# A short piece of rows moves from slot 23 to slot 10, and TensorE's loop is split in two around it

## The chip, the cores and the metric

The kernel runs on one core of one Trainium2 chip. The metric is device time in microseconds (us) for one execution. Four executions of the kernel before took 488.97, 487.42, 485.47 and 479.20 us, a median of 486.44. One further execution was profiled: it took 480.64 us, of which the span from the first to the last instruction is 478.9 us.

## The reference

A grouped 1x1 convolution over a 512 x 512 image of 192 channels in bfloat16: four groups of 48 channels, each multiplied by its own 48 x 48 matrix. With a kernel size of 1 there is no padding and one term in the sum:

```
x: (1, 512, 512, 192) bf16        w: (1, 1, 4, 48, 48) bf16
xg  = x.reshape(1, 512, 512, 4, 48)
out = einsum('bhwgc,gcd->bhwgd', xg, w[0, 0]).reshape(1, 512, 512, 192)
```

So 262,144 pixels of 192 channels are read, 100.7 MB, and as many bytes are written. Each pixel is independent of every other, which leaves the order free.

## The kernel before, in words

**Pieces and slots.** The pixels are cut into pieces (`plan_pieces`, L73). A full piece holds 128 rows, one per partition, and a number of columns; a column is one pixel of 192 channels, 384 bytes. Most pieces have 80 columns, so each partition's part is one contiguous run of 30,720 bytes. The work unit is a *group* of 4 columns, and two groups make a *pair*; there are 513 groups and 257 pairs. Pieces lie in 26 *slots*: slot 0 holds three small pieces (8, 24 and 48 columns), slots 1 to 22 and slot 24 one piece of 80 columns each, slot 25 one of 68, and slot 23 the *short piece*. That one has 64 columns and only 120 rows: partitions 16 to 19 and 48 to 51 are left out of it (`PARTIAL`, L40), so nothing is read into them or written from them. It is made of five blocks of rows: two of 16 rows, moved by the same queues as the other pieces (SP for loads, ACT for stores), and three of 44, 12 and 32 rows, moved by POOL. Ahead of the first two of these, POOL issues a tiny *fill* transfer (L234) into a tile that nobody reads.

**The rings.** Loaded columns lie in `ring`, three slots of 80 columns. A slot's load is issued when TensorE has transposed the piece that lay there three slots earlier (`freed`, L210; waits at L238 for POOL and L258 for SP). Results lie in `oring`, 280 columns, written round and round. Where a full piece would run over the end, its store is split in two; the short piece is not split: where it doesn't fit before the end, it starts at column 0 (L108). Before ScalarE writes a group into `oring`, it waits until the store that last read those columns has landed (`landed`, L356, called at L384).

**The engines.** TensorE transposes each group's 4 columns with six 128 x 128 transposes (L291, into `xT_ps`), one pair ahead of the matmuls that multiply them with the block-built weights `wt` (L311, six for each group, into `o_ps`). VectorE copies a pair's transposes to SBUF (L349). ScalarE copies each group's result to `oring` (L386) and issues the store of a finished piece (L367) when it comes to the second group after it; then for the short piece it also tells POOL to issue its three stores (L369). SP issues all other loads (L260) in the order of the pieces. The tail is cut finer: pieces with fewer than 240 columns behind them are stored in parts of 40, the last one in parts of 24, 20, 16 and 8.

**TensorE's program.** Its code is written out pair by pair, apart from one hardware loop (L333). A loop body is 60 groups, or 30 pairs: three slots, after which all buffers and semaphores repeat. `loop_span` (L117) finds the run of 80-column pieces that begins with slot 1; the loop starts at pair 10 and makes 7 rounds, and pairs 220 to 256 follow, written out. The short piece ends the run, since its loads have other semaphores. The programs of VectorE and ScalarE are written out in full.

Of the kernel before, what the change touches and what calls it, by code (L numbers as in the profile page):

```python
# [24 lines left out]
BIG = 80  # L25
SLOTS = 3
RCOLS = SLOTS * BIG
# [5 lines left out]
NXP = 4  # L33
NXS = 3
NOB = 4
NTOK = 6
# [5 lines left out]
    ("pool", 52, 44, 11), ("pool", 20, 12, 3), ("pool", 96, 32, 8),  # L42
)
PARTIAL_COLS = 64
PARTIAL_SLOT = 23

FILL_ROWS = 5
FILL_BEFORE = (2, 3)
# [24 lines left out]
def plan_pieces(npix):  # L73
    few = PARTIAL_COLS * sum(b[2] for b in PARTIAL)
    partial = npix >= few + 128 * BIG * PARTIAL_SLOT
    cols = (npix - few * partial) // 128
    assert cols % 4 == 0
    head = list(HEAD) if cols >= sum(HEAD) else []
    mid = cols - sum(head)
    slots = [[(BIG, FULL)]] * (mid // BIG) + ([[(mid % BIG, FULL)]] if mid % BIG else [])  # L80
    if head:
        slots.insert(0, [(s, FULL) for s in head])
    if partial:
        slots.insert(PARTIAL_SLOT, [(PARTIAL_COLS, PARTIAL)])
    pieces, g, pix = [], 0, 0
    for n, parts in enumerate(slots):
        c = n % SLOTS * BIG
        for s, blocks in parts:
            pieces.append(Piece(len(pieces), n, c, g, s, blocks, pix))
            c, g, pix = c + s, pieces[-1].g1, pieces[-1].pix_end  # L90
    assert pix == npix
    return pieces
# [21 lines left out]
    return stores  # L114


def loop_span(pieces, ng):  # L117

    body = RCOLS // 4
    a = next((p.g0 for p in pieces if p.slot == 1), ng)  # L120
    b = a
    for p in pieces:
        if p.slot >= 1 and p.g0 == b and p.full and p.size == BIG:
            b = p.g1

    rounds = max(0, (b - a - 2) // body)
    return a, body, rounds


def bass_standalone__grouped__vision_kernel(nc, x, w, out):  # L130
# [5 lines left out]
    pieces = plan_pieces(npix)  # L136
# [2 lines left out]
    store_of = {g: s for s in stores for g in range(s.g0, s.g1)}  # L139
    NG = pieces[-1].g1  # L140
    NP = (NG + 1) // 2
    LA, LB, LR = loop_span(pieces, NG)
    assert LA % 2 == 0 and LB % (2 * NXS) == 0 and LB % (2 * NTOK) == 0 and LB % NXP == 0

    xf = x.rearrange("b h w c -> (b h w) c")
    of = out.rearrange("b h w c -> (b h w) c")
# [2 lines left out]
    def groups(pair):  # L149
        return range(2 * pair, min(2 * pair + 2, NG))  # L150
# [21 lines left out]
    with ExitStack() as es:  # L172
# [27 lines left out]
        def columns(g):  # L200
            p = piece_of[g]
            at = p.at + 4 * (g - p.g0)
            return ring[:, at * C:(at + 4) * C]
# [58 lines left out]
        @block.tensor  # L262
        def _(pe):

            def build_weights():
                pe.wait_ge(e_sem, 1)
                pe.wait_ge(w_sem, 16)
                last = None
                for (tc, r, g, c0_) in WBLOCKS:
                    s0 = ESHIFT - r  # L270
                    col = WOFF[tc] + c0_
                    last = pe.matmul(o_ps[:, NOB - 1, col:col + CG], lhsT=esel[:, s0:s0 + 128],  # L272
                                     rhs=w_sb[:, g, :], start=True, stop=True, skip_group_check=True)
                last.then_inc(wb_sem, 1)

            def transposes(pair):
                todo = []
                for g in groups(pair):
                    p = piece_of[g]
                    if g % 2 and pair:  # L280
                        pe.wait_ge(e_done[(pair - 1) % NTOK], 1)
                    if g == p.g0:
                        keys = [ld_key[p.i, n] for n in range(len(p.blocks))]
                        for key in keys:
                            pe.wait_ge(ld_sem[key], 16)
                        todo += keys if p.full else []
                    xg = columns(g)
                    for ul in range(2):
                        for tc in range(3):
                            j = ul * 3 + tc  # L290
                            last = pe.transpose(xT_ps[:, g % NXP, j * 128:(j + 1) * 128],  # L291
                                                xg[:, j * 128:(j + 1) * 128], ident[:])
                            if todo and 0 < j < 5:
                                last.then_inc(ld_sem[todo.pop(0)], -16)
                assert not todo
                last.then_inc(t_done, 1)

            def matmuls(pair):
                if pair + 1 == NP or len(groups(pair + 1)) < 2:
                    pe.wait_ge(e_done[pair % NTOK], 1)  # L300
                for g in groups(pair):
                    xs = xT_sb[pair % NXS][:, g % 2 * 2 * UC:(g % 2 + 1) * 2 * UC]
                    if g >= 2:
                        pe.wait_ge(fa_done[(g - 2) % (2 * NTOK)], 1)
                    last = None
                    for ul in range(2):
                        v = 2 * g + ul
                        for tc in range(3):
                            j = ul * 3 + tc
                            c0_, c1_ = COLR[tc]  # L310
                            last = pe.matmul(o_ps[:, v % NOB, c0_:c1_], lhsT=xs[:, j * 128:(j + 1) * 128],  # L311
                                             rhs=wt[:, WOFF[tc]:WOFF[tc] + (c1_ - c0_)],
                                             start=(tc == 0), stop=(tc == 2), skip_group_check=True)
                            if j == 2 and g >= 2:
                                last.then_inc(fa_done[(g - 2) % (2 * NTOK)], -1)
                            if j == 1 and g % 2 == 0:
                                last.then_inc(e_done[pair % NTOK], -1)
                    last.then_inc(mm_done, 1)

            def step(pair):  # L320
                if pair + 1 < NP:
                    transposes(pair + 1)
                matmuls(pair)

            build_weights()
            pe.wait_ge(id_sem, 1)
            transposes(0)
            pe.wait_ge(wc_sem, 1)
            first = LA // 2 if LR > 1 else NP
            for pair in range(first):  # L330
                step(pair)
            if LR > 1:
                with pe.Fori(0, LR):  # L333
                    for pair in range(first, first + LB // 2):
                        step(pair)
                for pair in range(first + LR * LB // 2, NP):
                    step(pair)

        @block.vector
        def _(dve):  # L340
# [80 lines left out]
```

## Time and profile before

| | us |
|---|---|
| median of four executions | 486.44 |
| lowest, highest | 479.20, 488.97 |
| the profiled execution | 480.64 |
| its span | 478.9 |
| busy TensorE matmul, ScalarE, VectorE in it | 427.7, 388.9, 246.3 |
| bytes moved, mean rate over the span | 201.65 MB, 421 GB/s |
| median from issue to landing: an 80-column load, an 80-column store | 26.2, 45.1 |

The profile page cuts the span into 40 slices of 12.0 us. A digit is the busy share of a slice in tenths, and 9 stands for 90% or more. TensorE's matmuls are pipelined and the ends of their records are modelled, so its busy time is no measure of how close it is to its peak. The row of the DMA engines is the mean over sixteen. A wait in the views below names the engine and line that stood idle, what it was released by, the total in us, the number of such waits and the longest. In the view of stages each engine's busy time comes with its count of instructions, and "PEclk" is the share of TensorE's clock that was granted.

### The profile page before, as it was taken

The page shows a single profiled execution, that of the slowest core. Times are in us where ns is not written, and L with a number is a line of the kernel's source. Part 1 is how long each engine was busy: PE and PEld are TensorE (multiplying, and loading weights), DVE is VectorE, ACT ScalarE, POOL GpSimd, SP SyncE. Part 2 cuts the span into 40 slices and gives each one's busy share as a digit, 9 for nine tenths or more (in the row PEclk, how much of TensorE's full clock was granted, in tenths as well). Part 3 has the DMA queues.
Part 4 walks back from the last instruction along what each step waited for, and adds up shares of the span by engine and source line. Part 5 has one row for each costly group of instructions (what it writes and reads, how often), then busy time and mean ns, then how long its engine had stood idle before and what let it go on. Part 6 is the DMA issues. An engine that isn't in the chain of part 4 may idle for free.

```text
span 478.9 us, 13531 instructions
## 1 busy us (share of the span) xinstructions
PE 427.7 (89%) x6166; PEld 386.8 (81%) x6166; DVE 246.3 (51%) x258; ACT 388.9 (81%) x514; POOL 7.0 (1%) x18
## 2 busy tenths in 40 slices
PE   5999999999969989989999299999998988988993
PEld 4888888888869879879888288888887877877882
DVE  2555555555535535544555235555554544545452
ACT  2999999999959878878899289998897977977994
POOL 1000000000000000000000000000000020000200
PEclk9999999999989999998999789999999999999998
DMA  8999999999999999999999999999999999999996
GB/s 328 441 417 419 436 417 446 420 432 431 436 434 427 439 421 439 423 436 431 417 416 441 421 431 428 429 426 436 421 436 437 421 417 424 421 431 417 425 401 273
DMA packets 9991, 201.65 MB, mean 421 GB/s; under 512 B 1664, under 2 KB 1664, under 8 KB 2432
## 3 DMA queue, kind: packets, MB, share of 16 engines
q1 hardware_dynamic: 4136, 98.52, 48.4%
q10 hardware_dynamic: 5224, 98.50, 48.2%
q0 software_dynamic: 608, 4.33, 2.2%
q8 instruction: 14, 0.23, 0.2%
q14 instruction: 9, 0.07, 0.0%
HBM read 100.68 MB, written 100.66 MB: 420 GB/s over the span
## 4 chain that ended last, share of the span: by engine, by line
PE 47%; DMA 38%; ACT 9%; another core or an unknown queue 2%; issue 1%; ACTq 1%; POOL 0%; SPq 0%
DMA out_dram<-oring 29%; PE o_ps L311 28%; PE xT_ps L291 20%; DMA ring<-in_x_dram 9%; ACT oring L386 9%; ACTq L367 1%; POOL fill L234 0%; POOL ring L241 0%; SPq L260 0%; SPq L253 0%; ACTq L360 0%; ACTq L369 0%
## 5 line engine op out<-in xcount | busy, mean ns | idle before, releaser
L386 ACT CAST oring<-o_ps 128x768 bf16<-128x768 f32 x513 | 387.6, 801 | 84.1 <-PE o_ps L311 45.0
L349 DVE COPY xT_sb<-xT_ps 128x1536 bf16<-128x1536 bf16 x257 | 245.7, 956 | 220.8 <-PE xT_ps L291 220.8
L311 PE MATMUL o_ps<-wt,xT_sb 128*128 128x144 bf16 (+1 forms) x3078 | 288.6, 236 | 37.3 <-ACT oring L386 33.1
L311 PEld LDWEIGHTS o_ps<-wt,xT_sb 128*128 128x128 bf16 x3078 | 212.4, 99 | 74.9 <-ACT oring L386 66.5
L291 PE MATMUL xT_ps<-ident,ring 128*128 128x128 bf16 x3078 | 220.3, 221 | 5.0 <-DMA ring<-in_x_dram 5.0
L291 PEld LDWEIGHTS xT_ps<-ident,ring 128*128 128x128 bf16 x3078 | 187.9, 99 | 8.2 <-issue 5.6
L234 POOL DMA_DIRECT2D fill<-in_x_dram x4 | 2.4, 598 | 438.1 <-PE xT_ps L291 382.0
L272 PE MATMUL o_ps<-w_sb,esel 48*128 48x48 bf16 x10 | 0.6, 209 | 2.6 <-DMA w_sb<-in_w_dram 2.6
L272 PEld LDWEIGHTS o_ps<-w_sb,esel 48*128 48x128 bf16 x10 | 0.4, 111 | 2.6 <-POOL esel L220 2.6
L342 DVE CAST wt<-o_ps 128x480 bf16<-128x480 f32 x1 | 0.7, 658 | 3.2 <-PE o_ps L272 3.2
L386 ACT ACT_TABLE_LOAD x1 | 1.3, 1283 | 0.8 <-PEq L406 0.8
L241 POOL DMA_DIRECT2D ring<-in_x_dram x3 | 1.7, 564 | 0.0
L247 POOL DMA_DIRECT2D out_dram<-oring x3 | 1.7, 556 | 0.0
L220 POOL TENSOR_SCALAR_AFFINE_SELECT esel<-esel 48x272 bf16<-48x272 bf16 x1 | 0.4, 402 | 0.0
L217 POOL MEMSET esel<- 48x272 bf16 x1 | 0.3, 318 | 0.3 <-POOLq L406 0.3
L224 POOL TENSOR_SCALAR_AFFINE_SELECT ident<-ident 128x128 bf16<-128x128 bf16 x1 | 0.3, 282 | 0.0
L218 POOL MEMSET ident<- 128x128 bf16 x1 | 0.2, 198 | 0.0
L406 POOL MEMSET const-float32-0.0<- 128x1 f32 x1 | 0.1, 99 | 0.3 <-issue 0.3
L406 POOL MEMSET const-bfloat16-1.0<- 128x1 bf16 x1 | 0.1, 102 | 0.0
L406 POOL MEMSET const-uint8-127<- 128x1 uint8 x1 | 0.1, 102 | 0.0
L406 POOL MEMSET const-float32-1.0<- 128x1 f32 x1 | 0.1, 99 | 0.0
## 6 DMA issues: line engine op xcount, KB each, us to landing
ring<-in_x_dram SPq DMA_DIRECT2D x23, 3840.0 KB, 26.2
out_dram<-oring ACTq DMA_DIRECT2D x18, 3840.0 KB, 45.1
out_dram<-oring ACTq DMA_DIRECT2D x9, 1920.0 KB, 42.4
out_dram<-oring ACTq DMA_DIRECT2D x3, 1152.0 KB, 11.4
ring<-in_x_dram SPq DMA_DIRECT2D x1, 3264.0 KB, 25.8
ring<-in_x_dram SPq DMA_DIRECT2D x1, 2304.0 KB, 10.8
out_dram<-oring ACTq DMA_DIRECT2D x1, 2304.0 KB, 27.6
out_dram<-oring ACTq DMA_DIRECT2D x4, 384.0 KB, 9.9
```

The source lines that it names most:

```text
L220: gp.affine_select(out=esel[:], in_=esel[:], pattern=[[-1, ECOLS]], compare_op=AluOpType.is_equal, fill=0.0, base=ESHIFT, channel_multipli ...
L234: gp.dma_start(dst, src).then_inc(fill_sem[k], 16)
L241: gp.dma_start(sbuf, dram).then_inc(ld_sem[ld_key[p.i, n]], 16)
L247: gp.dma_start(dram, sbuf).then_inc(st_sem[i][n], 16)
L272: last = pe.matmul(o_ps[:, NOB - 1, col:col + CG], lhsT=esel[:, s0:s0 + 128], rhs=w_sb[:, g, :], start=True, stop=True, skip_group_check=True)
L291: last = pe.transpose(xT_ps[:, g % NXP, j * 128:(j + 1) * 128], xg[:, j * 128:(j + 1) * 128], ident[:])
L311: last = pe.matmul(o_ps[:, v % NOB, c0_:c1_], lhsT=xs[:, j * 128:(j + 1) * 128], rhs=wt[:, WOFF[tc]:WOFF[tc] + (c1_ - c0_)], start=(tc == ...
L342: dve.tensor_copy(wt[:], o_ps[:, NOB - 1, 0:WCOLS]).then_inc(wc_sem, 1)
L349: dve.tensor_copy(xT_sb[pair % NXS][:, 0:n * 2 * UC].rearrange("p (g c) -> p g c", g=n), xT_ps[:, b0:b0 + n, 0:2 * UC]).then_inc(e_done[pa ...
L367: act.dma_start(dram, sbuf).then_inc(st_sem[i][n], 16)
L386: act.copy(out_columns(g).rearrange("p (u c) -> p u c", u=2), o_ps[:, v % NOB:v % NOB + 2, 0:UC]).then_inc(fa_done[g % (2 * NTOK)] if g < ...
L406: nc = _bacc.Bacc("TRN2", target_bir_lowering=False, num_devices=1)
```

## The change

The constant `PARTIAL_SLOT` goes from 23 to 10, so slots 1 to 9 and 11 to 24 hold the 80-column pieces, slot 10 the short piece, and slot 25 still 68 columns. The number of groups and of pixels in each piece stays the same. The slots' places in the two rings shift behind slot 10; in `oring` the short piece would now begin at column 240, where its 64 columns don't fit, and starts at 0. There are 39 stores in place of 37, since splits fall elsewhere.

`loop_spans` replaces `loop_span` and finds every run of 80-column pieces. TensorE's program becomes: pairs 0 to 8 written out, a loop of 30 pairs with 3 rounds (pairs 9 to 98), pairs 99 to 106 written out (the short piece and its neighbours), a loop of 30 pairs with 4 rounds (107 to 226), and pairs 227 to 256 written out. The loops' bodies do what they did before.

```diff
-PARTIAL_SLOT = 23
+PARTIAL_SLOT = 10
...
-def loop_span(pieces, ng):
-
-    body = RCOLS // 4
-    a = next((p.g0 for p in pieces if p.slot == 1), ng)
-    b = a
-    for p in pieces:
-        if p.slot >= 1 and p.g0 == b and p.full and p.size == BIG:
-            b = p.g1
-
-    rounds = max(0, (b - a - 2) // body)
-    return a, body, rounds
+def loop_spans(pieces):
+
+    body, out, run = RCOLS // 4, [], []
+    for p in pieces + [None]:
+        if p and p.full and p.size == BIG:
+            run.append(p)
+            continue
+        if run:
+
+            first = max((run[0].g0 - 1) // 2, 1)
+            rounds = (run[-1].g1 - 2 * first - 2) // body
+            if rounds > 1:
+                out.append((first, body // 2, rounds))
+        run = []
+    return out
...
-            first = LA // 2 if LR > 1 else NP
-            for pair in range(first):
+            pair = 0
+            for first, body, rounds in LOOPS:
+                for pair in range(pair, first):
+                    step(pair)
+                with pe.Fori(0, rounds):
+                    for pair in range(first, first + body):
+                        step(pair)
+                pair = first + rounds * body
+            for pair in range(pair, NP):
                 step(pair)
-            if LR > 1:
-                with pe.Fori(0, LR):
-                    for pair in range(first, first + LB // 2):
-                        step(pair)
-                for pair in range(first + LR * LB // 2, NP):
-                    step(pair)
```

More of the change, by code (lines that the diff above doesn't have):

```diff
@@ L141, in bass_standalone__grouped__vision_kernel @@
     NP = (NG + 1) // 2
-    LA, LB, LR = loop_span(pieces, NG)
-    assert LA % 2 == 0 and LB % (2 * NXS) == 0 and LB % (2 * NTOK) == 0 and LB % NXP == 0
+    LOOPS = loop_spans(pieces)
+    assert all(RCOLS // 4 % n == 0 for n in (2 * NXS, 2 * NTOK, NXP))
     xf = x.rearrange("b h w c -> (b h w) c")
```

## The prediction

> **What bounds the kernel now.** I read the slices of the page first, then the stages, the waits of ACT, and last the landing times of the stores.
>
> ```profile
> PEclk9999999999989999998999789999999999999998
> DMA  8999999999999999999999999999999999999996
> ...
> q8 instruction: 14, 0.23, 0.2%
> ...
> DMA out_dram<-oring 29%; PE o_ps L311 28%; PE xT_ps L291 20%; DMA ring<-in_x_dram 9%; ACT oring L386 9%; ACTq L367 1%; POOL fill L234 0%; POOL ring L241 0%; SPq L260 0%; SPq L253 0%; ACTq L360 0%; ACTq L369 0%
> ```
>
> The DMA row is full in 38 of 40 slices, and the shares of the queues (48.4, 48.2, 2.2 and 0.2%) add up to 99.0% of sixteen engines. The chain's largest share is a store on its way. Stage by stage (columns: length, then busy PE, PEld, DVE, ACT, POOL with counts, clock, DMA share, GB/s):
>
> ```profile
> 20.00:110.00 90.00, 88.22 (x1310) 80.14 (x1308) 52.43 (x55) 81.99 (x109) 0.00 (x0) 1.00 1.00 427
> 110.00:390.00 280.00, 252.00 (x3611) 228.07 (x3608) 144.63 (x152) 226.46 (x301) 2.93 (x5) 0.96 1.00 429
> 390.00:450.00 60.00, 52.83 (x774) 47.56 (x774) 29.98 (x32) 49.35 (x66) 2.75 (x5) 1.00 1.00 425
> 450.00:479.00 29.00, 20.72 (x296) 18.18 (x294) 11.77 (x13) 20.68 (x28) 0.00 (x0) 0.92 0.84 350
> ```
>
> From 20 to 450 us the transfers leave nothing over; only the last 29 us hold idle DMA time, 0.16 x 29 = 4.6 us. Compute is faster than the transfers: ACT takes 20 groups in 16.5 us where nothing stops it (group 20 at 26.8 us, group 40 at 43.3), while the stores of neighbouring 80-column pieces land 18.1 us apart. So it must stand still somewhere, and it does at L384, for old stores:
>
> ```profile
> ACT oring L386 <- DMA out_dram<-oring: 29.7, 11, 9.3
> ...
> PE xT_ps L291 <- DMA ring<-in_x_dram: 5.0, 3, 2.0
> ...
> 274.84 1.50 ACT L386 CAST oring<-o_ps 128x768 bf16<-128x768 f32 x2 [9.31 <-DMA out_dram<-oring]
> ...
> 275.69 1.78 PE L311 MATMUL o_ps<-wt,xT_sb 128*128 128x144 bf16 x12 [8.85 <-ACT oring L386]
> ```
>
> Which part of a store is late? The trace records each transfer's sixteen completion increments, and I read them as one per DMA engine. Median and last increment of a store, in us: slot 2, 89.7 and 91.3; slot 5, 153.2 and 157.0; slot 7, 189.3 and 194.8; slot 13, 289.5 and 305.7; second half of slot 17, 369.4 and 389.6; slot 21, 437.5 and 446.9; the very last, 476.8 and 478.4. One increment falls behind alone: between the stores of slots 14, 15 and 16 the medians are 18.2 and 18.1 us apart, the last ones 19.0 and 18.9, some 0.8 us or 4% more. The 9.31 us above end 0.1 us after slot 11's last increment (274.76). The lag goes away around the 120-row piece: slot 24's first load, issued behind it, lands with its median at 391.0 and its last at 392.2. The piece leaves out rows 16-19 and 48-51 in both directions, 16 row packets of 24,576 B. A 30,720 B packet takes 1.138 us, so these are 16 x 0.91 = 14.6 us. I take it that these are the slow engine's.
>
> [...]
>
> **The change, part by part.** The sum is made against the profiled execution: 480.64 us, of which the span is 478.9, so 1.74 lies around it. The median of the runs shown is 486.44, 5.8 above it, and I add that at the end.
>
> *More straight code on TensorE.* Straight pairs were 10 + 30 (loop body) + 37 = 77 and become 9 + 30 + 8 + 30 + 30 = 107. 77 pairs came as 14 code blocks of 16,384 B, 5.5 pairs each, so 30 more pairs are 6 more blocks. A block's packet takes 0.88 to 0.97 us (13.1 us for all 14), together 5.6 us of one engine's time: 0.35 us if spread over sixteen, 5.6 if all fall on the engine that ends last. The 7 blocks fetched from 16.7 to 69.7 us would alone have put one engine 6.6 us behind; no increment is over 1.7 us late by then. So spread: +0.35.
>
> *Loop rounds.* 7 rounds become 3 + 4, jumps back 6 become 5. In before the first jump comes near 76 us, and PE is busy 16.01 us of 60:76.5 against 16.20 of the next 16.5 us: at most 0.2 us, hidden under compute's 30 us of waiting. Zero. [...]
>
> *The piece's loads.* POOL's fills and three loads, and SP's two small ones, now wait for pair 80 (slot 7 transposed) instead of 210. SP is past that wait at 144.3 us; nothing else is queued on POOL, and SP's next load waits for slot 8 anyway. Before, the five took from 383.6 to 423.9 us, and PE stood for the last:
>
> ```profile
> ring<-in_x_dram POOLq DMA_DIRECT2D x1, 768.0 KB, 37.6
> ...
> 424.02 0.83 PE L291 MATMUL xT_ps<-ident,ring 128*128 128x128 bf16 x12 [2.00 <-DMA ring<-in_x_dram]
> ```
>
> With the same 40.3 us it lands at 184.6, about 1 us after PE would want group 200 (ACT takes it at 185.7). Covered by the next item.
>
> *The output ring.* Slot 10 would start at column 240, where 64 columns do not fit; it starts at 0, and 40 columns stay unused in that turn. Group 200 then waits for slot 7's store (189.3 median, 194.8 last) instead of slot 6's (175.9): PE stands 4 to 9 us from 185.7. Behind this wait, on ACT, is slot 9's store, issued only with group 201; SP's next load comes later too. Cover: at 186 us slot 12's load (issued 182.0) and slot 8's store (165.8) are still ahead, up to 2 x 8 x 1.138 = 18 us of each engine's time. So nothing; with the cover gone, up to 9.
>
> *The relief comes early.* By slot 10 the slow engine is about 5.5 us behind; 14.6 us less work put it 9 us ahead by some 230 us. At 4% it loses about 10.5 us over the remaining 250 us and ends about 1.5 us behind, as now (478.4 against 476.8). Its work is the same, so the move alone is worth nothing unless it runs out of queued work while ahead. In between ACT no longer waits 10 to 20 us for one engine.
>
> *The end of the run.* The 2.0 us at 424 and the 1.71 us that ACT idled at 442.7 behind the piece's two own stores (issue 1.90 us) leave a stretch where compute sets the pace; slot 17's 20 us lag, after which group 420 could start only at 389.6, leaves too. What is late next is the DMA itself: 99.0 to 99.2% of 478.9 is 474.1 to 475.1 us of work; take 474.9 (the packets' times, 7,598 us over sixteen), +0.35, + 1.6 idle in the first 20 us (share 0.92), + a drain I put at 1.3 (bounds 0.5 and the present 4.6): 478.1. Two more stores on ACT (39 for 37, 0.34 us issue each) hide under its waits.
>
> Sum: 478.1 + 1.74 = 479.8, that is 0.8 below 480.64; against the median, **485.6 us**.
>
> **Rivals.** *The relief is lost (slower).* While ahead, the slow engine may empty its queue and wait for issues; each idle us is 1 us at the end, since its lag grows again to the last store. Place: about 210 to 300 us. It decides once the lead exceeds that engine's queued work. For it: slot 9's store comes 9 us later. Against: typically one load and over two stores are outstanding (26 and 45 us to landing). At most the 9 us lead is lost: 486.4 - 0.8 + 9 = 494.7. Both this and the uncovered ring wait together would pass 2%.
>
> *Compute behind the slow engine sets the slower executions (faster).* Runs spread from 479.2 to 488.97. If the upper ones come from a longer wait for the lagging store near 390 us, with compute in the open from there, all fall to the DMA's floor: 479.8. For it: from 389.6 to 473.1 us the chain is nearly all PE and ACT. Against: if the engine is simply slower in those runs, its total is the bound in both kernels.
>
> *The slow engine isn't the one relieved, or nothing waits for it*: then only code blocks and drain differ, 480.64 + 0.35 or 486.8.
>
> **How the numbers follow.** Forecast 0.50, no effect 0.12, faster 0.20, relief lost 0.18. Medians of a few runs can differ by half of the spread shown. The range goes from 477.5 (floor, with the drain at its least and 1 us of spread) to 494.7. 2% is about what a measurement of this kernel can tell from no change: under 476.7 I give 0.06 (the floor would have to fall too), over 496.2 0.12 (relief lost with the ring wait, or code blocks all on the late engine), the rest 0.82.
>
> **What would show it.** PE's 2 us before 424 gone; a wait of 4 to 9 us in ACT at 186 to 195; last increments of stores not behind the median from 230 to 400, then a few us; 20 code blocks instead of 14, six of them between 180 and 250; DMA share in the last 29 us over 0.9. Wrong if DMA slices after 200 us fall below 9, if code blocks repeat each round, or if the lag is the same as before.

## The result: 0.2% slower, where a small gain was forecast

| | executions | median us | lowest, highest |
|---|---|---|---|
| before | 74 | 482.11 | 478.65, 488.97 |
| changed | 48 | 483.22 | 480.17, 491.02 |

The ratio is 1.0021, with a 95% interval of 1.0006 to 1.0036: 1.0 us more, between 0.3 and 1.7. The forecast was 0.8 us less. The time lies in the range and within 2%, but it moved the other way. The 5.8 us that the forecast added for the difference between the profiled execution and the median came from four executions; with 74 the difference is 1.5.

The first profiled execution of the changed kernel was a long one, 489.93 us, and such executions occur with both kernels. So the lines below are from another profiled execution of the same kernel, 479.75 us, with a span of 478.0, beside the 480.64 us of before. It lies 3.5 us under its own kernel's median; two more, 483.14 and 483.70 us, stand beside it where they differ. Its page, from the slices, the queues and the chain:

```profile
PEclk9999999999988996899999999999999888999998
DMA  8999999999999999999999999999999999999997
...
q8 instruction: 20, 0.33, 0.2%
...
DMA out_dram<-oring 27%; PE o_ps L315 27%; PE xT_ps L295 20%; ACT oring L391 10%; DMA ring<-in_x_dram 9%; ACTq L372 1%; POOL fill L238 0%; POOL ring L245 0%; POOL out_dram L251 0%; SPq L264 0%; SPq L257 0%; ACTq L365 0%; ACTq L374 0%
```

The DMA engines are as full as before (the shares of the queues add up to 99.2%, where they were 99.0), and TensorE's code takes 20 blocks, as forecast. Seven of the blocks come between 194 and 252 us, behind slot 10. The stages (columns as in the prediction):

```profile
20.00:110.00 90.00, 88.23 (x1311) 80.21 (x1310) 51.84 (x55) 82.12 (x110) 0.00 (x0) 1.00 1.00 427
110.00:390.00 280.00, 253.09 (x3629) 230.40 (x3627) 144.58 (x151) 228.18 (x303) 5.68 (x10) 0.96 1.00 428
390.00:450.00 60.00, 56.02 (x802) 50.67 (x799) 32.06 (x34) 50.66 (x68) 0.00 (x0) 0.97 1.00 426
450.00:478.00 28.00, 18.96 (x270) 16.69 (x270) 10.62 (x12) 18.97 (x26) 0.00 (x0) 0.93 0.88 368
```

Here compute is further ahead at the end: TensorE has 18.96 us of work left after 450 us, where it had 20.72, and the last stage idles 0.12 x 28 = 3.4 us of DMA time instead of 4.6. That is what the forecast expected of the end. But the two executions near the median don't show it. From 450 to 477 us they read:

```profile
450.00:477.00 27.00, 23.14 (x334) 20.39 (x331) 13.01 (x14) 22.73 (x30) 0.00 (x0) 1.00 0.93 388
...
450.00:477.00 27.00, 23.05 (x333) 20.31 (x329) 13.01 (x14) 22.64 (x30) 0.00 (x0) 1.00 0.91 383
```

TensorE has 23.1 us of work left there, more than before, and up to the end of their spans (481.4 and 482.0 us) the DMA share is 0.85 and 0.83, so 4.7 and 5.4 us idle. Back to the execution of 479.75 us, its waits, and the one that stands out:

```profile
ACT oring L391 <- DMA out_dram<-oring: 16.9, 6, 5.3
...
PE xT_ps L295 <- DMA ring<-in_x_dram: 11.4, 3, 8.5
...
188.62 1.44 PE L295 MATMUL xT_ps<-ident,ring 128*128 128x128 bf16 x12 [8.52 <-DMA ring<-in_x_dram]
...
ring<-in_x_dram POOLq DMA_DIRECT2D x1, 768.0 KB, 39.6
```

ACT waits 16.9 us for old stores instead of 29.7. In exchange, TensorE waits 8.52 us for the short piece's loads before slot 10.

### The profile page after: what moved, and what is told of

The parts are those of the page before. It is cut to its first block, busy times and chain, and to the rows that moved or that the text cites. A ratio compares the mean times of both kernels' runs of the same rounds, so it can differ in the third digit from the quotient of the medians.

```text
span 488.2 us, 13536 instructions
## 1 busy us (share of the span) xinstructions
PE 431.3 (88%) x6166; PEld 391.7 (80%) x6166; DVE 246.3 (50%) x258; ACT 389.4 (80%) x514; POOL 7.0 (1%) x18
## 4 chain that ended last, share of the span: by engine, by line
PE 46%; DMA 38%; ACT 10%; another core or an unknown queue 2%; issue 1%; POOL 1%; ACTq 1%; SPq 0%
DMA out_dram<-oring 28%; PE o_ps L315 27%; PE xT_ps L295 19%; ACT oring L391 10%; DMA ring<-in_x_dram 10%; ACTq L372 1%; POOL fill L238 0%; POOL ring L245 0%; POOL out_dram L251 0%; SPq L264 0%; SPq L257 0%; ACTq L365 0%; ACTq L374 0%
## 5 line engine op out<-in xcount | busy, mean ns | idle before, releaser
L315 PEld LDWEIGHTS o_ps<-wt,xT_sb 128*128 128x128 bf16 x3078 | 215.0, 100 | 70.2 <-ACT oring L391 61.8
L295 PE MATMUL xT_ps<-ident,ring 128*128 128x128 bf16 x3078 | 222.8, 223 | 12.4 <-DMA ring<-in_x_dram 12.4
L295 PEld LDWEIGHTS xT_ps<-ident,ring 128*128 128x128 bf16 x3078 | 190.4, 100 | 15.5 <-issue 13.0
## 6 DMA issues: line engine op xcount, KB each, us to landing
ring<-in_x_dram SPq DMA_DIRECT2D x1, 3264.0 KB, 18.1
```

## The experiments

Two theories at first. **CODE**: the six more blocks of TensorE's code cost the time. **LEAD**: the slow DMA engine, relieved early, gets ahead, runs out of queued work there and so loses part of the relief. Here and below an engine is late or early by what one of a store's sixteen increments shows, taken as one per engine; in the kernel before, one of them falls behind by 0.8 us from store to store at slots 14 to 16, 4% of 18.1. A third came up on the way, **SKIP**: the 40 columns that the output ring leaves out at slot 10. "Short piece in slot N" below is the changed kernel with that one constant. All of them have 107 straight pairs and 20 code blocks, so the amount of code is the same; with the place, the points where the ring splits stores in two move as well (38 to 41 stores). Ratios are against executions of the kernel before on the same chip.

### The changed kernel again

No edit; it ran beside each of the first, second and fourth groups.

> The changed kernel again, beside the next three on one chip. Both theories expect 1.001 to 1.004 of the kernel before. Theory CODE (the six more blocks of TensorE's code cost the time) expects that the last increments of the closing stores stand behind their medians by no more than before, 1.6 to 4 us. Theory LEAD (the slow engine does not keep the lead that the early relief gives it) expects them 5 us or more behind the medians at 460 to 475 us, and the DMA engines idle in the last 25 us for longer than the 4.6 us of before.

> The changed kernel once more, beside slots 4 and 16 on one chip: 1.001 to 1.004 of the kernel before. LEAD expects it below slot 4 and above slot 16; if only code counts, the three are alike within their intervals; if the skipped columns cost, it is above both.

> The changed kernel beside slots 7, 11 and 17 on one chip: 1.001 to 1.004. LEAD expects the order 7, 10, 11, 17 from dear to cheap; with the skip as the cause, 10 and 17 are dearest.

Measured: 1.0029 (0.9996 to 1.0061), 1.0017 (0.9980 to 1.0054) and 0.9982 (0.9952 to 1.0012), with medians 483.17, 483.38 and 483.13 us, within 0.3 us of each other. The third ratio lies under all that was expected, though its median is like the others': the ratio of one and the same kernel moved by 0.5% between groups, and differences of 0.2% between single ratios decide nothing. The last increment of the last store stands 2.7, 2.1 and 2.7 us behind its median (1.6 before). Between 460 and 475 us LEAD's mark of 5 us is reached in the third profiled execution only (5.3; at most 2.8 and 4.2 in the others, 4.5 before). Neither theory's mark is clear in this kernel alone, and the tests need a larger lever.

### Code: the split loop alone, and no loop at all

The changed program generator with the short piece back in slot 23:

```diff
-PARTIAL_SLOT = 10
+PARTIAL_SLOT = 23
-    LOOPS = loop_spans(pieces)
+    LOOPS = [(10, 30, 3), (108, 30, 4)]
```

> The short piece stays in slot 23, TensorE's program is cut as in the changed kernel: loops of 3 and 4 rounds with 8 written-out pairs between them, 107 straight pairs, 20 code blocks expected. CODE expects the whole loss here, 1.002 of the kernel before (0.35 to 1.0 us). LEAD expects 1.000 to 1.001.

> Slot 23 with 107 straight pairs a second time: CODE from the kernel without loops (3.1 us for 34 blocks) gives 0.55 us for 6, 1.001; first measured 1.0007.

And with `LOOPS = []`:

> The short piece in slot 23, TensorE's program without any loop: 257 straight pairs, some 47 code blocks, 33 more than before. CODE, at 1 us for 6 blocks, expects 5.5 us more: 1.011. If blocks cost only their share of sixteen engines (0.93 us each, spread), 33 x 0.93 / 16 = 1.9 us: 1.004. LEAD expects that second figure or less.

Measured: 1.0007 (0.9974 to 1.0039) and 0.9997 (0.9967 to 1.0027) with the split loop; 1.0065 (1.0038 to 1.0092) without a loop. The queue of TensorE's code in the kernel without a loop:

```profile
q8 instruction: 48, 0.79, 0.6%
```

The kernel without a loop has no jumps back either; if those are free, 34 blocks cost 3.1 us (1.8 to 4.4), and six would cost 0.55 (0.32 to 0.78). That is a little over the 0.35 of the forecast, which the split loop at slot 23 doesn't contradict. CODE's first form, 1 us for six blocks, expected 1.011 and is out. By this estimate, 0.55 of 1.0 us, code accounts for about half of the change's loss; the split loop alone shows none of it.

### No short piece

`partial = False` in `plan_pieces` of the kernel before: all rows of all pieces are moved, POOL moves nothing, and the work in all is the same.

> The kernel before without any short piece: 24 pieces of 80 columns and one of 48 after the head, all of 128 rows, one loop, no POOL transfers. If one slow engine in sixteen is what the short piece relieves and it bounds the end, its 14.6 us come back there: the last increments of the closing stores alone lag by 10 us or more, and the time is 1.02 to 1.03 of the kernel before. If the slow engine isn't the one relieved, or its lag is harmless, 0.995 to 1.002.

Measured: 1.0154 (1.0102 to 1.0206). The last stores: median 484.0, second-to-last increment 484.0, last 486.8 us; at 471.8 us the last stands 12.1 us behind its median. One engine ends alone, 2.8 us behind the second-to-last increment, and from 450 to 487 us the DMA share is 0.68:

```profile
450.00:487.00 37.00, 25.74 (x374) 22.82 (x372) 14.61 (x16) 25.53 (x34) 0.00 (x0) 0.88 0.68 286
```

The short piece does relieve the late engine, and it is worth 7.4 us, half of the 14.6 us that the packets left out of it would take; the time lies under the 1.02 to 1.03 that was expected for it. The "isn't the one relieved" rival falls.

### The place: slots 4 to 19

> The short piece in slot 4, at about 75 us, when the slow engine is only 1.5 us behind; 107 straight pairs as in the changed kernel (one loop of 6 rounds), no columns skipped in the output ring. LEAD, if the lead is partly lost, expects more than at slot 10: 1.005 to 1.02, with the last increments of the closing stores alone 5 us or more behind. If an engine's lead is kept whole, only the code blocks differ: 1.001.

> The short piece in slot 7 (about 125 us), loops of 2 and 5 rounds, 107 straight pairs, no columns skipped. LEAD: between slot 4 (1.0082) and slot 11 (1.0014), about 1.005, with DMA time of one engine idle soon after the piece's stores. If the skipped columns are what slot 10 pays, no more than 1.002.

> The short piece in slot 11 with loops on both sides: it starts at column 40 of the output ring, so no 40 columns are skipped, and its first group waits for an older store than in the changed kernel. If the skip (and the pause of PE near 187 us) costs the time, 1.000 of the kernel before; CODE and LEAD expect 1.001 to 1.004, as in the changed kernel.

> Slot 11, no skip, a second time (first 1.0014): LEAD expects 1.000 to 1.002, a little under slot 10. If the skip costs, 0.998, like slot 13.

> The short piece in slot 13 (about 235 us), 107 straight pairs, no columns skipped. LEAD: the slow engine is then 7 to 9 us behind, so it gets 6 to 7 us ahead, less than the 9 us of slot 10; the value lies between slot 10 (1.002) and slot 16 (0.995): 0.998. If the position has no price and slot 16's 0.9953 was chance, 1.001.

> The short piece in slot 16, at about 290 us; loops of 5 and 2 rounds, 107 straight pairs again, no columns skipped. LEAD expects a value between that of slot 23 with the same code (1.0007 measured) and slot 10 (1.002 to 1.003); if only code counts, 1.001.

> Slot 16 a second time, on another draw of runs: LEAD expects 0.993 to 0.998 again; if the first value was chance, 1.001.

> The short piece in slot 17, loops of 5 and 2 rounds, 107 straight pairs; as in slot 10 the piece does not fit behind column 240 of the output ring and 40 columns are skipped. LEAD: as slots 16 and 19, 0.995 to 0.999. If the skip costs, 0.4% above them: 1.001 to 1.003.

> The short piece in slot 19 (about 340 us), 107 straight pairs (one loop of 6 rounds), no columns skipped. LEAD: the slow engine is 12 us or more behind, so it hardly gets ahead and loses nothing; what is late then is the store for which ACT waits before the relief. 0.995 to 0.999.

The last column is DMA time without work between 20 and 440 us, in us of one engine, summed from the trace's packets over all stretches of more than 20 ns with fewer than sixteen in flight. The trace doesn't say which engine moved a packet. Several values are several profiled executions.

| short piece in slot | skip in the output ring | ratio (95% interval) | median us | out of work |
|---|---|---|---|---|
| 4 | no | 1.0082 (1.0048 to 1.0115) | 486.99 | 8.1 |
| 7 | no | 1.0113 (1.0062 to 1.0163) | 486.49 | 0.5 |
| 10, the change | **yes** | 1.0021 (1.0006 to 1.0036) | 483.22 | 0.9, 3.1, 3.5 |
| 11 | no | 1.0014 (0.9975 to 1.0052), 0.9984 (0.9950 to 1.0018) | 482.35, 481.52 | 1.3, 0.5 |
| 13 | no | 0.9981 (0.9950 to 1.0012) | 481.09 | 0.0 |
| 16 | no | 0.9953 (0.9915 to 0.9992), 0.9985 (0.9962 to 1.0008) | 481.04, 481.09 | 0.8, 0.1 |
| 17 | **yes** | 1.0022 (0.9998 to 1.0046) | 482.85 | 5.1 |
| 19 | no | 0.9989 (0.9962 to 1.0017) | 481.31 | 0.0 |
| 23, 20 blocks | no | 1.0007, 0.9997 | 481.55, 482.26 | 1.2, 0.7 |
| 23, the kernel before | no | 1 | 482.11 | 0.2 |

Two things stand in it. First, too early is dear: slots 4 and 7 cost 4 to 5 us (slot 7 on six executions only, spread from 483.01 to 492.55). Stages of slot 4:

```profile
80.00:100.00 20.00, 18.34 (x244) 17.13 (x245) 9.49 (x10) 14.13 (x19) 0.00 (x0) 0.85 1.00 429
100.00:120.00 20.00, 17.87 (x268) 16.19 (x266) 10.62 (x12) 16.89 (x23) 2.75 (x5) 1.00 0.97 404
...
450.00:486.00 36.00, 21.10 (x301) 18.45 (x298) 12.05 (x13) 21.04 (x28) 0.00 (x0) 0.85 0.71 295
```

Between 100 and 120 us the DMA share falls to 0.97, mostly with fifteen packets in flight. One engine is through with the piece's stores at 108.5 us, when the middle ones of the sixteen have 8 to 20 us to go, and stands without work. At the end the last increment is alone 8.8 us behind its median (485.7 against 476.9), 7.2 us more than before, beside 8.1 us out of work: the lost lead has come back as lag. That is LEAD, shown at slot 4. At slot 7 the time agrees, but its profiled execution (483.0 us, 3.5 below its median) hardly shows an engine out of work, so there the cause stays open.

Second, slots 10 and 17 stand out between their neighbours: 17 is 1.5 to 1.8 us above 16 and 19 in the medians, 10 is 0.9 to 1.7 above 11. They are the two with a skip. The gaps are small: in the group that ran 10 and 11 a second time their ratios, 0.9982 and 0.9984, are alike. LEAD alone does not explain them: at slot 11 the early engine leads by 13 us and more (median minus first increment, stores from 254 to 334 us) and hardly ever runs out of work.

### The skip alone

Only the column at which the first store begins is changed. At slot 10 the short piece then begins at column 0 by itself; at slot 16 it would begin at 240 and 40 columns are skipped.

```diff
 PARTIAL_SLOT = 10
-    stores, at = [], 0
+    stores, at = [], 40
```

> The changed kernel with the output ring's first store at column 40: the short piece in slot 10 then begins at column 0 without a skip, everything else alike. If the skip costs: 0.996 to 1.000 of the kernel before, about 1.2 to 1.9 us under the changed kernel (median 483.2), like slots 11 and 13. If the place costs (LEAD): 1.002, as the changed kernel.

```diff
-PARTIAL_SLOT = 10
+PARTIAL_SLOT = 16
-    stores, at = [], 0
+    stores, at = [], 80
```

> Slot 16 with the ring's first store at column 80: the piece would begin at column 240 and 40 columns are skipped, everything else as in the kernel with slot 16 (0.9953 and 0.9985). If the skip costs: 1.000 to 1.003, 1.2 to 1.9 us more, as slot 17. If not: 0.995 to 0.999.

Measured: slot 10 without the skip 0.9942 (0.9908 to 0.9976), median 480.66 us; slot 16 with it 1.0023 (0.9997 to 1.0049), median 483.47. The second is as expected for a skip that costs; the first is a little under the 0.996 to 1.000 expected. The skip taken from slot 10 is worth 2.6 us in the medians, and put into slot 16 it costs 2.4; by the ratios it is 3.8 us, and 1.8 or 3.4 against the two runs of slot 16. Stages of slot 16 with the skip, from the piece's stores on:

```profile
300.00:330.00 30.00, 21.47 (x298) 19.95 (x299) 11.50 (x12) 17.56 (x24) 2.76 (x5) 0.83 1.01 428
330.00:340.00 10.00, 9.91 (x152) 9.02 (x149) 5.75 (x6) 9.21 (x13) 0.00 (x0) 1.00 0.95 377
340.00:360.00 20.00, 19.67 (x295) 17.91 (x293) 11.61 (x13) 18.28 (x25) 0.00 (x0) 1.00 1.01 414
```

and of slot 16 without it:

```profile
290.00:320.00 30.00, 23.34 (x309) 21.43 (x306) 12.61 (x14) 18.70 (x25) 0.00 (x0) 0.89 1.00 427
320.00:330.00 10.00, 8.59 (x129) 7.93 (x130) 4.75 (x6) 8.68 (x12) 2.75 (x5) 1.00 1.00 424
330.00:350.00 20.00, 19.48 (x291) 17.64 (x289) 11.45 (x13) 18.11 (x25) 0.00 (x0) 1.00 1.00 426
```

With the skip there are 10 us at a DMA share of 0.95 and 377 GB/s, while PE, ACT and DVE run; without it none of the stretches shown is below 1.00, and no 10 us from 290 to 360 us below 0.98 or 419 GB/s. Out of work, in us of one engine: 4.5 with and 0.1 without at slot 16; 0.6 without at slot 10, where the changed kernel had 0.9 to 3.5.

What follows: the skip costs, and with it goes work from the DMA queues. The pair at slot 10 is the cleanest. Both kernels have 39 stores, and from the short piece on all stores have the same columns and the same places in the ring; ahead of it the places in the ring differ, and slot 6's store is split in two instead of slot 3's. (The three repeats of the changed kernel ran on other chips, each beside the kernel before.) At slot 16 the splits behind the piece move as well (38 stores for 39), and between slots 16, 17 and 19 too, so a part of those 2.4 and 1.5 to 1.8 us may be theirs.

How exactly the skip costs is argued, not shown. By the plan of the stores, it brings ACT's waits closer: the first ten groups of the short piece and of each of the next two pieces wait for the store of a piece that ended 40 groups earlier, where without the skip it is 60. So less can be queued for one turn of the ring, while one engine is ahead.

The short piece in slot 10 with the ring's first store at column 40 beats both kernels: 0.58% under the kernel before (0.24 to 0.92%), 2.6 us under the changed kernel's median. Its waits, and its last stage:

```profile
ACT oring L391 <- DMA out_dram<-oring: 24.3, 5, 8.1
PE xT_ps L295 <- DMA ring<-in_x_dram: 6.5, 4, 2.6
...
450.00:478.00 28.00, 18.71 (x269) 16.44 (x267) 10.29 (x12) 18.64 (x25) 0.00 (x0) 0.90 0.88 370
```

The wait for the short piece's loads shrinks to 2.6 us at most, and the last stage is like that of the changed kernel.

## Why the prediction was right or wrong

**What bounds the kernel**: right. Between 20 and 440 us no kernel of the table had more than 8.1 us of one engine's time without work, of 16 x 420; one engine is late, by up to 20.2 us in the kernel before (389.6 against 369.4), and without the short piece one ends alone (1.0154). One row was misread: 391.0 and 392.2 us are the increments of POOL's first fill. Slot 24's load is issued at 404.2 and lands at 428.6, its last increment at 431.4, and the stores still lag by 10 us there and by 1.6 at the very end. So the lag goes away by the end of the run, not at once.

***The output ring*: this step failed.** It costed the skip at nothing, "so nothing; with the cover gone, up to 9", since up to 18 us of each engine's time were still queued at 186 us. The runs price it, by the medians, at 2.6 us in slot 10 itself, and at 1.5 to 2.4 in slots 17 and 16. The step looked for cover at the one moment of the wait; the lack shows later, 30 to 100 us after it in the changed kernel (stretches at 220, 250 and 270 to 290 us), mostly with one engine of sixteen out of work. That this idle time is what the skip costs was not shown apart. With 1.5 to 2.6 us in place of nothing the forecast's -0.8 becomes +0.7 to +1.8; +1.0 (0.3 to 1.7) was measured.

***The piece's loads***: landing was forecast for 184.6 us and came at 186.4 to 188.5, but TensorE wanted them at 179 or 180, not 1 us before they were due, so it waits 7.6 to 8.5 us, not 1. This is where the wait forecast for ACT in the ring's step went: ACT's waits there, 9.74 us in the execution of 479.75 us and 8.82 in that of 483.70, end with TensorE's matmuls and not with a store. That it costs nothing agrees with slot 11, which has the same wait, 7.6 and 7.7 us, with ratios of 1.0014 and 0.9984.

***More straight code***: 20 blocks, right; +0.35 us forecast, 0.55 (0.32 to 0.78) by the kernel without loops, within the interval of 1.0007 and 0.9997. ***Loop rounds***: not tried alone, but the five jumps are in both slot 23 kernels too, and cost nothing to be seen there. In the kernel before no code block is fetched between 69.7 and 410.7 us, while its loop jumps back six times.

***The relief comes early***: "worth nothing unless it runs out of queued work" was right for slot 10, by the kernel without the skip, and the rival's loss is real: at slot 4 it is 0.8%, with 8.1 us out of work. That the 14.6 us of packets left out are all the late engine's was an assumption, and so were the 9 us ahead that followed from it: no trace names the engine of a packet. What the runs showed in its place is a first increment 13 us and more ahead of the median at slot 11, and a time 7.4 us longer without the short piece. The price of 9 us was too high: 4 to 5 us at slots 4 and 7. The forecast put its point of decision between 210 and 300 us, and there the changed kernel's stretches without work lie. "In between ACT no longer waits 10 to 20 us for one engine" came out in one execution only; in the two near the median ACT stood 8.6 and 10.0 us for the short piece's last store on POOL (2.2 in that of 479.75 us, 5.7 without the skip):

```profile
261.48 0.80 ACT L391 CAST oring<-o_ps 128x768 bf16<-128x768 f32 x1 [9.98 <-DMA out_dram<-oring]
```

***The end of the run***: -0.8 with the code was right in sign and about in size, but not for this kernel: with as many code blocks, slots 11 to 19 without a skip gave 1.0014, 0.9984, 0.9981, 0.9953, 0.9985 and 0.9989, on average 0.8 us less. Slot 10 without the skip gave 0.9942, 2.8 us less, and why it gained so much more stays open. That the gain comes from the end of the run was not tested apart. In the sum, the packets in the span add up to 7,588 us, not 7,598, which makes that term 474.3 for 474.9. The drain of 1.3 us was a guess: the last 28 to 32 us hold 3.4, 4.7 and 5.4 us of idle DMA time in the three executions.

**The faster rival**, all executions at the DMA's floor, did not come: the changed kernel's go up to 491.02 us. **The marks**: code blocks right, the 2 us at 424 gone; a DMA share over 0.9 in the last 29 us missed narrowly in one execution (0.88; 0.84 before) and clearly in the two near the median (0.85 and 0.83); the last increments of 80-column stores from 265 to 400 us lag by 2 to 5 us in that one and by 8 to 12 in the two others, which was not foreseen, and its cause stays open.

## What to carry to other kernels

In this kernel, with a DMA share of 1.00 from 20 to 450 us, what is queued mattered more than who waits: a pause of TensorE of 7.6 us cost nothing that can be seen (slot 11), while 40 columns less in the output ring cost 1.5 us or more. When a piece is moved along a ring, look where its new place falls in the ring, and look for the least queued work of a single DMA engine, not of the mean. Relief for one slow engine came too early at slot 4, where that engine was hardly behind (1.6 us at slot 2's store in the kernel before) and 8.1 us of one engine's time were without work; from slot 11 on, without a skip, it was at most 1.3 us.

## What the runs showed of the hardware

In the kernel before, one of the sixteen increments falls behind by 4% of the time (0.8 us of the 18.1 between the stores of slots 14 to 16); the kernel with no short piece to make up for it took 7.4 us longer. Without loops TensorE's 34 more code blocks cost 0.09 us each if the jumps back are free, against 0.06 if a packet's 0.94 us (the mean of the 14 in the kernel before) were spread over sixteen engines. And after its pause at 188.62 us TensorE took 1.44 us for twelve transposes that take 0.83 before it; in the kernel before it took 1.49 at 277.27 us, behind a pause of 8.85 that ended at 275.69.
